# Two attention blocks on one core: gates loaded as one row, first K and V side by side, other buffers and leads, and the last outputs partly projected ahead

## The chip, the cores and the metric

The kernel runs on one core of one Trainium2 chip. The metric is device time in microseconds (us). The kernel before takes 1134.37 us (median of 3 runs, 1133.22 to 1134.79).

The engines are TensorE (PE in the profile; PEld is its weight load), ScalarE (ACT), VectorE (DVE), GpSimd (POOL) and SyncE (SP), which issues most of the DMAs (289 of the 292 in the trace before).

## The reference

Two blocks are computed and their outputs stand side by side, 2048 rows of 1024 each. There are 32 heads of width 32.

```python
# A: plain softmax attention over 2048 keys
qkv = x @ wqkv
p = softmax(q @ k.T * Dh**-0.5);  a = (p @ v) @ wo
# B: 4 segments of 512; causal softmax inside a segment, plus a memory M, z of earlier segments
g = sigmoid(beta)                                  # one gate per head
a_dot = softmax(qs @ ks.T * scale + mask) @ vs
a_mem = (phi(qs) @ M) / (phi(qs) @ z + 1e-6)
o = g * a_mem + (1 - g) * a_dot;  b = concat(o) @ wo
```

## The kernel before

A small list scheduler in Python decides, before the program is built, the order of instructions on every engine. A unit is one query block of 256 rows of one group of four heads (A), or one segment of one group (B). Each unit is cut into score batches: TensorE writes scores into two of three pairs of PSUM banks, and ScalarE takes the exponential of a pair (128x1024) at a time. "Position" (`pos`) counts score batches, and other work is due at a position. The two remaining PSUM banks (`side`) serve everything else: projections, PV and output tiles. PV is the product of the exponentials with V.

```python
par = dict(b=(12, 7, 2), ..., ob=1, lead=5, wob=60, oks=(0, 3), sh=2, od=8, run=6, ...)

def load_misc(self):                       # the gates
    for h in range(4):
        src = bass.AP(tensor=self.B_beta.tensor, offset=self.B_beta.offset + h, ap=[[0, 32], [4, NG]])
        ... e.dma_start(self.beta[32 * h:32 * h + 32, 0:NG], src)      # 32x8 elements of 2 bytes
    yield do("ACT", lambda e: e.activation(gB, self.beta[:, :], ACTF.Exp, scale=-1.0), ...)
    ...

def pv_unit(self, u, steps, half):
    if not self.first_pv:
        self.first_pv = True
        yield ("ev", ("ex", u, 1))         # the first PV goes after two batches of exponentials
    ...
    OB, = yield acq(self.side, 1, -1000)   # and holds a side bank from here on
    ...

def out_A(self, qb):                       # output projection of a query block
    ...                                    # waits for the last two groups of that block
    for tt in range(2):
        for half in range(2):              # 4 tiles of 128x512, 8 groups = 32 matmuls each
            self.Q.spawn(self.out_rows(...))
```

Of the kernel before, what the change touches and what calls it, by code (L numbers as in the profile page):

```python
# [17 lines left out]
NG = 8  # L18
# [153 lines left out]
class Sched:  # L172
# [31 lines left out]
    def step(self, gen, val):  # L204
        while True:
            try:
                req = gen.send(val)
            except StopIteration:
                self.nproc -= 1
                return  # L210
            k = req[0]
            if k == "do":
                rq = req[1]
                rq.proc = gen
                self.seq += 1
                rq.seq = self.seq
                self.q[rq.eng].append(rq)
                self.kick(rq.eng)
                return
            if k == "acq":  # L220
                pool, n, prio, pick = req[1:]
                got = self.take(pool, n, pick)
                if got is not None and not any(x[0] < prio for x in pool.waiting):
                    val = got
                    continue
                if got is not None:
                    pool.items = got + pool.items
                    pool.items.sort()
                self.seq += 1
                pool.waiting.append((prio, self.seq, n, pick, gen))  # L230
                pool.waiting.sort(key=lambda x: x[:2])
                return
            if k == "ev":
                if req[1] in self.events and self.events[req[1]] is True:
                    val = None
                    continue
                self.events.setdefault(req[1], []).append(gen)
                return
            if k == "until":
                if req[1] <= self.now:  # L240
                    val = None
                    continue
                self.at(req[1], lambda g=gen: self.step(g, None))
                return
            raise ValueError(k)
# [10 lines left out]
    def give(self, pool, items):  # L256
        pool.items.extend(items)
        pool.items.sort()
# [119 lines left out]
class Kernel:  # L378
    par = dict(b=(12, 7, 2), mem=-2, memM=2, span=50, rate=0.58, ahead=28, sl=4, pv=24, ob=1, lead=5, b0=1, bpos=16, wob=60, mg=0.05, off=0, oks=(0, 3), sh=2, pd=4, o0=4, od=8, run=6, po=(1, 1), fp=2, fil=0.65, fs=0.15)
# [48 lines left out]
    def alloc(self):  # L428
# [36 lines left out]
        self.beta = sb("beta", [P, 8])  # L465
# [9 lines left out]
    def pt(self, slots):  # L475

        k = slots[0][0]
        i = [s[1] for s in slots]
        step = i[1] - i[0] if len(i) > 1 else 1
        t = (self.PT, self.WoBs, self.OTAs)[k]  # L480
        return t[:, i[0]:i[-1] + 1:step, :]

    def pkey(self, s):
        k, i = s
        if k == 0:
            return ("PT", i)
        return ("WoB", i // 2) if k == 1 else ("OTA", 2 + i // 4, i % 4)
# [14 lines left out]
    def load_xB(self, s):  # L502
        src = self.B_x[0][512 * s:512 * s + 512, :]
        yield do("SP", lambda e: e.dma_start(self.xB[:, :, :], src, transpose=True), w=["xB"], cost=5.2, prio=6, kb=1024)
        self.Q.fire(("xB", s))

    def load_misc(self):
        nc = self.nc
        for h in range(4):
            src = bass.AP(tensor=self.B_beta.tensor, offset=self.B_beta.offset + h, ap=[[0, 32], [4, NG]])  # L510

            def f(e, h=h, src=src):
                with nc.allow_non_contiguous_dma(reason="tiny beta broadcast"):
                    return e.dma_start(self.beta[32 * h:32 * h + 32, 0:NG], src)
            yield do("SP", f, w=[("beta", h)], cost=0.5, prio=8, kb=300)
        gA, gB = self.gcol[:, 0, :], self.gcol[:, 1, :]
        yield do("ACT", lambda e: e.activation(gB, self.beta[:, :], ACTF.Exp, scale=-1.0),
                 r=[("beta", h) for h in range(4)], w=["gcol"], cost=0.2, prio=9)
# [5 lines left out]
    def constants(self):  # L524
# [6 lines left out]
        yield pool(lambda e: e.memset(self.zero[:, :], 0.0), ["zero"])  # L531
        for i in range(2):
# [78 lines left out]
    def rest_x(self):  # L611
        yield ("ev", ("XS", 2))
        yield ("ev", ("XS", 3))
        for c in range(1, 4):
            for t in (0, 2):
# [3 lines left out]
                         r=[("XS", 3), ("XS", 2), ("XS", 1), ("XS", 0)] if c == 1 and t == 0 else [], w=[("xA", c, t), ("xA", c, t + 1)], cost=2.6, prio=1, kb=512)  # L619
# [3 lines left out]
    def job(self, due, mm, keys, out, okey, wkeys, scale=None, eng="DVE", cost=None, okeys=(), gate=None, n=512):  # L623
# [4 lines left out]
        for i in range(last + 1):  # L628
# [4 lines left out]
            if i == 0:  # L633
# [33 lines left out]
    def a_prep(self, g):  # L667
# [16 lines left out]
        if g == 0:  # L684
            todo[0:2] = [("K", 0, 0, 2), ("Q", 0, 0, 2), ("K", 0, 2, 4), ("Q", 0, 2, 4)]
        kind = {"K": 0, "Q": 1, "V": 2}
# [27 lines left out]
        if g == NG - 1:  # L714
            yield do("SP", lambda e: e.dma_start(self.WoA, self.A_wo.rearrange("(j p) n -> p j n", p=P)),
                     w=[("xA", c, t) for c in range(4) for t in range(4)], cost=0.6, prio=5, kb=2048)
            Q.fire("WoA")
        self.nA = g + 1
# [5 lines left out]
    def b_all(self):  # L724
        for n in range(32):
            if n % 8 == 0 and n:
                yield from self.load_xB(n // 8)
            yield from self.b_proj(n)

# [143 lines left out]
    def s_all(self):  # L873
# [6 lines left out]
        pr = yield acq(self.pairs, 1)  # L880
        Q.give(self.side, list(pr[0]))
        pr = yield acq(self.pairs, 1)
        Q.give(self.side, list(pr[0]))

    def s_batch(self, u, k):
# [49 lines left out]
        Q.fire(("pos", self.pos))  # L935
        for x in range(npair):
# [76 lines left out]
    def pv_unit(self, u, steps, half):  # L1013
        Q = self.Q
        if not self.first_pv:
            self.first_pv = True
            yield ("ev", ("ex", u, 1))
# [58 lines left out]
    def finish(self, u, half, OB, tb):  # L1076
# [7 lines left out]
        o = OD[:, 0:QU]  # L1084
        yield do("DVE", lambda e: e.tensor_copy(OD[:, :], self.ps[:, OB, :]), r=[("ps", OB)], w=[("OD", x), ("Rb", x)], cost=dve(2 * QU), prio=0,  # L1085
# [19 lines left out]
        if s == 0:  # L1105
            yield do("DVE", lambda e: e.scalar_tensor_tensor(dst, o, gB, Rb, ALU.mult, ALU.mult),
                     r=[("OD", x), ("Rb", x), "gcol"], w=[("OTB", g, half)], cost=dve(QU) + 0.08, prio=self.par["fp"])
            Q.give(self.ods, [x])
        else:
# [8 lines left out]
                     r=[("tB", tb), ("amem", b)], w=[("OTB", g, half)], cost=dve(QU), prio=self.par["fp"])  # L1118
# [6 lines left out]
    def out_rows(self, due, lhs, lkeys, W, wkey, row, col, gate=None):  # L1125
# [14 lines left out]
        yield do("SP", lambda e: e.dma_start(self.out[0][row:row + P, col:col + 512], self.outsb[ob][:, :]), r=[("outsb", ob)],  # L1140
# [3 lines left out]
    def out_A(self, qb):  # L1144
        yield ("ev", "WoA")
        last = qb == NQ - 1
        for g in (NG - 2, NG - 1):
            if last and g == NG - 1:
                yield ("ev", "s_done")
            else:  # L1150
                yield ("ev", ("fin", "A", g, qb))
        due = self.pos + 4
        for tt in range(2):
            for half in range(2):
                q0 = QU * qb + P * tt
                ns = slice(512 * half, 512 * half + 512)
                self.Q.spawn(self.out_rows(due, lambda j, q0=q0: self.OTA[:, j, q0:q0 + P],
                                           [[("OTA", j, qb // 2)] for j in range(NG)],
                                           lambda j, ns=ns: self.WoA[:, j, ns], [("xA", 0, 0)], q0, 512 * half,
                                           (NG - 1, ("fin", "A", NG - 1, qb)) if last else None))  # L1160
                due += 2
                yield ("until", self.Q.now)
# [199 lines left out]
    def main(self):  # L1362
# [19 lines left out]
        self.extra = [((1, 2 * i), (1, 2 * i + 1)) for i in range(8)] + [((2, 2 * i), (2, 2 * i + 1)) for i in range(8)]  # L1382
# [103 lines left out]
```

## Time and profile before

ScalarE bounds the kernel. These are two lines of the profile's page: the busy time of each engine with its share of the span and its instructions, and the costliest group (line, engine, operation, out<-in, shapes, count | busy, mean ns of one | idle time before them and what ended it).

```profile
PE 1052.7 (93%) x23589; PEld 514.0 (45%) x23589; DVE 720.3 (64%) x1463; ACT 1091.9 (96%) x1190; POOL 132.8 (12%) x286
...
L953 ACT ACTIVATE PT<-ps 128x1024 bf16<-128x1024 f32 x1168 | 1073.0, 1183 | 14.6 <-PE ps L926 14.5
```

With 16 more exponentials that go into borrowed tiles there are 1184. The mean of 1183 ns is the time of one from start to end. They overlap in the trace, where 245 in a row take 0.917 us each, so the cost of one is read from a run of them in the timeline. Below is the timeline of ScalarE before (start us, duration us, engine, line, operation, out<-in, count, and in brackets the idle time ahead of it with what ended it). Consecutive exponentials are merged; every bracket is a hole.

```profile
10.99 1.94 ACT L953 ACTIVATE WoB<-ps 128x1024 bf16<-128x1024 f32 x2 [7.35 <-PE ps L926]
...
42.55 1.94 ACT L953 ACTIVATE PT<-ps 128x1024 bf16<-128x1024 f32 x2 [1.56 <-PE ps L926]
47.14 7.44 ACT L953 ACTIVATE PT<-ps 128x1024 bf16<-128x1024 f32 x8 [2.65 <-PE ps L926]
55.01 5.61 ACT L953 ACTIVATE PT<-ps 128x1024 bf16<-128x1024 f32 x6 [0.44 <-PE ps L926]
62.11 0.21 ACT L517 ACTIVATE gcol<-beta 128x8 f32<-128x8 bf16 x1 [1.49 <-DMA beta<-in_B_beta_dram]
64.86 1.94 ACT L953 ACTIVATE PT<-ps 128x1024 bf16<-128x1024 f32 x2 [2.54 <-PE ps L926]
68.38 42.34 ACT L953 ACTIVATE PT<-ps 128x1024 bf16<-128x1024 f32 x46 [1.58 <-PE ps L926]
...
892.73 224.69 ACT L953 ACTIVATE PT<-ps 128x1024 bf16<-128x1024 f32 x245 [0.91 <-PE ps L926]
1118.91 0.59 ACT L1138 CAST outsb<-ps 128x512 bf16<-128x512 f32 x1 [1.49 <-PE ps L1132]
```

The last run has 245 exponentials in 224.69 us, 0.917 us each. At that pace 1184 exponentials need about 1086 us, and 1088.5 us are what is left of the span of 1132.8 without head, holes and tail. What can be won is the head up to 10.99 us, 17.92 us of holes, and the tail of 15.38 us after the last exponential, which ends at 892.73 + 224.69 = 1117.42 us.

The largest group of holes is at 60 to 68 us. There the timeline of TensorE before shows a stop in the middle of one projection (17 matmuls, then 3 of the next group):

```profile
58.83 1.24 PE L653 MATMUL ps<-xA,WA 128*32 128x512 bf16 x17
...
64.08 0.40 PE L653 MATMUL ps<-xA,WA 128*32 128x512 bf16 x3 [4.01 <-issue]
```

"issue" means that nothing the profile knows of released it. The DMA view of the kernel before for 56 to 60 us has many packets and no bytes to speak of:

```profile
DMA packets 452, 0.00 MB, mean 0 GB/s; under 512 B 452, under 2 KB 452, under 8 KB 452
```

Nearly all of them, 424 of the 452, are the gates: 1024 elements of 2 bytes in four loads, whose packets run from 52.1 to 61.7 us.

### The profile page before, as it was taken

The page shows a single profiled execution, that of the slowest core. Times are in us where ns is not written, and L with a number is a line of the kernel's source. Part 1 is how long each engine was busy: PE and PEld are TensorE (multiplying, and loading weights), DVE is VectorE, ACT ScalarE, POOL GpSimd, SP SyncE. Part 2 cuts the span into 40 slices and gives each one's busy share as a digit, 9 for nine tenths or more (in the row PEclk, how much of TensorE's full clock was granted, in tenths as well). Part 3 has the DMA queues.
Part 4 walks back from the last instruction along what each step waited for, and adds up shares of the span by engine and source line. Part 5 has one row for each costly group of instructions (what it writes and reads, how often), then busy time and mean ns, then how long its engine had stood idle before and what let it go on. Part 6 is the DMA issues. An engine that isn't in the chain of part 4 may idle for free.

```text
span 1132.8 us, 50803 instructions
## 1 busy us (share of the span) xinstructions
PE 1052.7 (93%) x23589; PEld 514.0 (45%) x23589; DVE 720.3 (64%) x1463; ACT 1091.9 (96%) x1190; POOL 132.8 (12%) x286
## 2 busy tenths in 40 slices
PE   7889999999899999999999999999999999999997
PEld 3444444444444444444444444444444444444444
DVE  2237556565784887979767876878567656663333
ACT  5889999999999999999999999999999999999995
POOL 1002102001111111111101201111111111110000
PEclk9999999999999999999999999999999999999999
DMA  9522622224121221254113232232213223211111
GB/s 182 100 46 58 132 54 59 48 55 90 45 45 34 63 59 45 49 69 91 48 40 58 45 60 48 49 77 54 52 42 67 46 40 66 73 22 36 39 40 52
DMA packets 214844, 67.32 MB, mean 59 GB/s; under 512 B 203872, under 2 KB 212064, under 8 KB 214624
## 3 DMA queue, kind: packets, MB, share of 16 engines
q1 hardware_dynamic: 213296, 63.20, 26.7%
q8 instruction: 187, 3.06, 1.2%
q10 hardware_dynamic: 1328, 0.79, 0.3%
q14 instruction: 33, 0.27, 0.1%
HBM read 36.70 MB, written 8.39 MB: 40 GB/s over the span
## 4 chain that ended last, share of the span: by engine, by line
ACT 82%; PE 11%; DVE 3%; DMA 1%; issue 1%; POOL 0%; DVEq 0%
ACT PT L953 81%; PE ps L653 4%; PE ps L1058 3%; PE ps L1132 2%; PE ps L926 2%; DMA VA<-VT 1%; DMA PKt<-PH 1%; DVE OD L1085 0%; ACT OTA L953 0%; PE ps L546 0%; DVE VT L659 0%; DVE we L988 0%; POOL PT L962 0%; ACT WoB L953 0%; DVE we L989 0%
## 5 line engine op out<-in xcount | busy, mean ns | idle before, releaser
L953 ACT ACTIVATE PT<-ps 128x1024 bf16<-128x1024 f32 x1168 | 1073.0, 1183 | 14.6 <-PE ps L926 14.5
L1058 PE MATMUL ps<-PT,ones 128*32 128x256 bf16 (+1 forms) x4800 | 294.7, 271 | 0.0
L1058 PE MATMUL ps<-PT,VA 128*32 128x256 bf16 x4032 | 252.9, 276 | 16.2 <-ACT PT L953 10.4
L926 PE MATMUL ps<-QA,KA 32*128 32x256 bf16 x4096 | 203.9, 273 | 31.9 <-ACT PT L953 22.8
L653 PE MATMUL ps<-xA,WA 128*32 128x512 bf16 (+1 forms) x3136 | 204.3, 378 | 8.5 <-issue 4.6
L653 PE MATMUL ps<-xB,WB 128*32 128x512 bf16 x3072 | 203.1, 381 | 1.1 <-DVE VT L659 0.3
L962 POOL TENSOR_SCALAR_AFFINE_SELECT PT<-PT 128x256 bf16<-128x256 bf16 (+1 forms) x224 | 104.0, 470 | 821.1 <-ACT PT L953 815.8
L926 PEld LDWEIGHTS ps<-QA,KA 32*128 32x128 bf16 x4096 | 60.9, 92 | 204.4 <-ACT PT L953 190.7
L1058 PEld LDWEIGHTS ps<-PT,VA 128*32 128x32 bf16 x4032 | 107.6, 96 | 87.0 <-issue 30.2
L1058 PEld LDWEIGHTS ps<-PT,ones 128*32 128x32 bf16 x4800 | 128.8, 97 | 25.1 <-issue 0.3
L653 PEld LDWEIGHTS ps<-xA,WA 128*32 128x32 bf16 x3136 | 72.9, 96 | 82.4 <-issue 29.0
L1138 DVE CAST outsb<-ps 128x512 bf16<-128x512 f32 x60 | 41.4, 689 | 100.0 <-PE ps L1132 99.9
L653 PEld LDWEIGHTS ps<-xB,WB 128*32 128x32 bf16 x3072 | 72.5, 96 | 70.0 <-issue 25.8
L1085 DVE COPY OD<-ps 128x512 f32<-128x512 f32 x128 | 87.3, 683 | 24.7 <-PE ps L1058 23.6
L659 DVE CAST KQB<-ps 128x512 bf16<-128x512 f32 x64 | 44.0, 688 | 76.1 <-PE ps L653 75.9
L659 DVE CAST VT<-ps 128x512 bf16<-128x512 f32 x64 | 44.0, 688 | 75.8 <-PE ps L653 73.0
L1132 PE MATMUL ps<-WoB,OTB 128*32 128x512 bf16 x1024 | 66.8, 381 | 0.1
L1132 PE MATMUL ps<-xA,OTA 128*32 128x512 bf16 x1024 | 65.6, 381 | 0.0
L1091 DVE STREAM_TRANSPOSE OD<-Rall 128x256 f32<-128x256 f32 x128 | 56.3, 441 | 3.4
L1088 DVE STREAM_TRANSPOSE Dt<-OD 128x256 f32<-128x256 f32 x128 | 55.8, 437 | 2.5
L1058 PE MATMUL ps<-PT,VB 128*32 128x256 bf16 (+1 forms) x768 | 45.6, 260 | 7.6 <-DVE OD L1085 3.8
L926 PE MATMUL ps<-KQB 32*128 32x128 bf16 (+3 forms) x512 | 43.0, 302 | 3.9 <-ACT PT L953 2.8
(77 smaller groups left out, 654.7 us busy)
## 6 DMA issues: line engine op xcount, KB each, us to landing
WB<-in_B_wk_dram SPq DMA_DIRECT2D x32, 256.0 KB, 2.9
WB<-in_B_wq_dram SPq DMA_DIRECT2D x32, 256.0 KB, 2.9
WB<-in_B_wv_dram SPq DMA_DIRECT2D x32, 256.0 KB, 3.3
out_dram<-outsb SPq DMA_DIRECT2D x64, 128.0 KB, 1.8
WA<-in_A_wqkv_dram SPq DMA_DIRECT2D x23, 256.0 KB, 3.2
WoB<-in_B_wo_dram SPq DMA_DIRECT2D x1, 2048.0 KB, 10.3
xA<-in_A_wo_dram SPq DMA_DIRECT2D x1, 2048.0 KB, 10.4
OTA<-in_A_x_dram ACTq DMA_DIRECT2D x2, 256.0 KB, 4.9
```

Source lines behind the costliest of these rows:

```text
L653: ins = e.matmul(self.ps[32 * c:32 * c + 32, bank, 0:n], W[:, i, 32 * c:32 * c + 32], x(i), start=(i == 0), stop=(i == NI - 1))
L659: return e.tensor_copy(dst, self.ps[:, bank, 0:n])
L926: ins = e.matmul(self.ps[:, bk, col:col + w], lhs(t, hs), rhs(q0, w, hs), start=True, stop=True)
L953: yield do("ACT", lambda e: e.activation(ap, self.ps[:, pr[0]:pr[1] + 1, :], ACTF.Exp, scale=sc), r=[("ps", bk) for bk in pr], w=keys, cos ...
L962: yield do("POOL", lambda e, m=m, n=n: e.affine_select(m, m, pattern=[[0, n], [1, P]], compare_op=ALU.is_ge, fill=0.0, base=0, channel_mul ...
L1058: ins = e.matmul(out, l, r, start=st, stop=sp)
L1085: yield do("DVE", lambda e: e.tensor_copy(OD[:, :], self.ps[:, OB, :]), r=[("ps", OB)], w=[("OD", x), ("Rb", x)], cost=dve(2 * QU), prio=0 ...
L1088: yield do("DVE", lambda e: e.transpose(Dt[:, :], Rb), r=[("Rb", x)], w=[("Dt", x)], cost=dve(QU), prio=self.par["fp"], hold=0.15)
L1091: yield do("DVE", lambda e: e.transpose(Rb.rearrange("p (a b) -> p a b", b=32), self.spread(Rc)), r=[("Rc", ui % 64)], w=[("Rb", x)], cost ...
L1132: ins = e.matmul(self.ps[32 * c:32 * c + 32, bank, :], lhs(j)[:, 32 * c:32 * c + 32], W(j), start=(j == 0), stop=(j == NG - 1))
L1138: return f(self.outsb[ob][:, :], self.ps[:, bank, :])
```

## The change

The intent is to take away what stands between ScalarE and its next exponential. The gates come as one row and TensorE spreads them. The first group's V projections run beside its K and Q projections, and the first PV waits until V is whole (`pvw`). B's projections are due earlier (`b`). Eight more places for exponentials (an exponential of 128x1024 takes two) are lent by B's output tile. Six of the last eight output tiles are projected over seven groups ahead of time into f32 partial sums, and only the last group is added at the end.

```diff
-    par = dict(b=(12, 7, 2), ..., ob=1, lead=5, wob=60, oks=(0, 3), sh=2, od=8, run=6, ...)
+    par = dict(b=(16, 12, 9), ..., ob=4, lead=6, wob=40, oks=(1,), sh=6, od=4, run=4, ..., ta=2, td=40, pvw=3)
@@ pools: first in, first out
-        pool.items.sort()
@@ load_misc
-        for h in range(4): ... four strided loads of 32x8 elements
+        yield do("SP", lambda e: e.dma_start(self.beta[0:1, :], self.B_beta.rearrange("(o h) -> o h", o=1)), ...)
+            for h in range(4):
+                ins = e.matmul(self.ps[32 * h:32 * h + 32, bank, 0:NG], self.ones32[:, :], self.beta[:, h:32:4], start=True, stop=True)
+        yield do("ACT", lambda e: e.activation(gB, self.ps[:, bank, 0:NG], ACTF.Exp, scale=-1.0), ..., prio=-2)
@@ a_prep
+        if g == 0:
+            streams = [[t for t in todo if t[0] != "V"], [t for t in todo if t[0] == "V"]]
@@ pv_unit
-            yield ("ev", ("ex", u, 1))
+            yield ("ev", ("VA", 0, self.par["pvw"]))
@@ main
+        self.extra = ... + [((3, 2 * i), (3, 2 * i + 1)) for i in range(4)]        # places in OTB
@@ finish: the last unit is normalised straight from PSUM
+        if u == ("A", NG - 1, NQ - 1): ...
@@ out_ahead (new): groups 0 to 6 now, group 7 later
+        yield from self.job(d, mm, ..., lambda e, bank, eng: e.tensor_copy(part, self.ps[:, bank, :]), [("part", i)] + over, ...)
+        yield ("ev", ("fin", "A", NG - 1, qb))
+        yield from self.job(-99, lambda e, j, bank: mm(e, NG - 1, bank, True), ...,
+                            lambda e, bank, eng: e.tensor_tensor(self.outsb[ob][:, :], self.ps[:, bank, :], part, ALU.add), ...)
```
(Cut: keys, costs, transfer sizes that only the scheduler's model uses, `out_A`'s choice of tiles, and one output DMA issued from ScalarE.)

More of the change, by code (lines that the diff above doesn't have):

```diff
@@ L257, in give @@
         pool.items.extend(items)
-        pool.items.sort()
         while pool.waiting:
@@ L378 @@
 class Kernel:
-    par = dict(b=(12, 7, 2), mem=-2, memM=2, span=50, rate=0.58, ahead=28, sl=4, pv=24, ob=1, lead=5, b0=1, bpos=16, wob=60, mg=0.05, off=0, oks=(0, 3), sh=2, pd=4, o0=4, od=8, run=6, po=(1, 1), fp=2, fil=0.65, fs=0.15)
+    par = dict(b=(16, 12, 9), mem=-2, memM=2, span=50, rate=0.58, ahead=28, sl=4, pv=24, ob=4, lead=6, b0=1, bpos=16, wob=40, mg=0.05, off=0, oks=(1,), sh=6, pd=4, o0=4, od=4, run=4, po=(1, 1), fp=2, fil=0.65, fs=0.15, ta=2, td=40, pvw=3)
     def __init__(self, nc, A_x, A_wqkv, A_wo, B_x, B_wq, B_wk, B_wv, B_wo, B_beta, out):
@@ L464, in alloc @@
         self.we = sb("we", [P, 512], F32)
-        self.beta = sb("beta", [P, 8])
+        self.beta = sb("beta", [P, 32])
         self.gcol = sb("gcol", [P, 2, 8], F32)
@@ L479, in pt @@
         step = i[1] - i[0] if len(i) > 1 else 1
-        t = (self.PT, self.WoBs, self.OTAs)[k]
+        t = (self.PT, self.WoBs, self.OTAs, self.OTB)[k]
         return t[:, i[0]:i[-1] + 1:step, :]
@@ L486, in pkey @@
             return ("PT", i)
+        if k == 3:
+            return ("OTB", i)
         return ("WoB", i // 2) if k == 1 else ("OTA", 2 + i // 4, i % 4)
@@ L503, in load_xB, with f @@
         src = self.B_x[0][512 * s:512 * s + 512, :]
-        yield do("SP", lambda e: e.dma_start(self.xB[:, :, :], src, transpose=True), w=["xB"], cost=5.2, prio=6, kb=1024)
+        yield do("SP", lambda e: e.dma_start(self.xB[:, :, :], src, transpose=True), w=["xB"], cost=5.2, prio=6, kb=1500)
         self.Q.fire(("xB", s))
     def load_misc(self):
-        nc = self.nc
-        for h in range(4):
-            src = bass.AP(tensor=self.B_beta.tensor, offset=self.B_beta.offset + h, ap=[[0, 32], [4, NG]])
-            def f(e, h=h, src=src):
-                with nc.allow_non_contiguous_dma(reason="tiny beta broadcast"):
-                    return e.dma_start(self.beta[32 * h:32 * h + 32, 0:NG], src)
-            yield do("SP", f, w=[("beta", h)], cost=0.5, prio=8, kb=300)
+        yield do("SP", lambda e: e.dma_start(self.beta[0:1, :], self.B_beta.rearrange("(o h) -> o h", o=1)), r=["beta0"], w=["beta"], cost=0.5,
+                 prio=8, kb=10)
+        bank, = yield acq(self.side, 1, self.first[("B", 0)])
+        def f(e):
+            for h in range(4):
+                ins = e.matmul(self.ps[32 * h:32 * h + 32, bank, 0:NG], self.ones32[:, :], self.beta[:, h:32:4], start=True, stop=True)
+            return ins
+        yield do("PE", f, r=["beta", "ones32"], w=[("ps", bank)], cost=0.1, prio=8, mode=COL)
         gA, gB = self.gcol[:, 0, :], self.gcol[:, 1, :]
-        yield do("ACT", lambda e: e.activation(gB, self.beta[:, :], ACTF.Exp, scale=-1.0),
-                 r=[("beta", h) for h in range(4)], w=["gcol"], cost=0.2, prio=9)
+        yield do("ACT", lambda e: e.activation(gB, self.ps[:, bank, 0:NG], ACTF.Exp, scale=-1.0), r=[("ps", bank)], w=["gcol"], cost=0.25, prio=-2)
+        self.Q.give(self.side, [bank])
         yield do("DVE", lambda e: e.tensor_scalar(gB, gB, 1.0, None, ALU.add), r=["gcol"], w=["gcol"])
@@ L531, in constants @@
         yield pool(lambda e: e.memset(self.zero[:, :], 0.0), ["zero"])
+        yield pool(lambda e: e.memset(self.beta[:, :], 0.0), ["beta0"])
         for i in range(2):
@@ L618, in rest_x @@
                 yield do("SP", lambda e, q0=q0, src=src: e.dma_start(self.xA[:, :, q0:q0 + 2 * P], src, transpose=True),
-                         r=[("XS", 3), ("XS", 2), ("XS", 1), ("XS", 0)] if c == 1 and t == 0 else [], w=[("xA", c, t), ("xA", c, t + 1)], cost=2.6, prio=1, kb=512)
+                         r=[("XS", 3), ("XS", 2), ("XS", 1), ("XS", 0)] if c == 1 and t == 0 else [], w=[("xA", c, t), ("xA", c, t + 1)], cost=2.6, prio=1, kb=680)
             self.Q.fire(("xA", c))
@@ L632, in job @@
                      prio=(lambda: self.jprio(due)) if i == 0 else (lambda: min(self.jprio(due), self.par["run"])), mode=COL)
-            if i == 0:
+            if i == 0 and last:
                 self.under.add(bank)
@@ L685, in a_prep, with a_stream @@
             todo[0:2] = [("K", 0, 0, 2), ("Q", 0, 0, 2), ("K", 0, 2, 4), ("Q", 0, 2, 4)]
+        if g == 0:
+            streams = [[t for t in todo if t[0] != "V"], [t for t in todo if t[0] == "V"]]
+        else:
+            streams = [todo]
+        for i, st in enumerate(streams):
+            Q.spawn(self.a_stream(g, st, due, ("stream", g, i)))
+        for i in range(len(streams)):
+            yield ("ev", ("stream", g, i))
+        if g == NG - 1:
+            yield do("SP", lambda e: e.dma_start(self.WoA, self.A_wo.rearrange("(j p) n -> p j n", p=P)),
+                     w=[("xA", c, t) for c in range(4) for t in range(4)], cost=0.6, prio=5, kb=2048)
+            Q.fire("WoA")
+        self.nA = g + 1
+    def a_stream(self, g, todo, due, done):
+        Q = self.Q
+        b = g % 2
         kind = {"K": 0, "Q": 1, "V": 2}
@@ L713, in a_prep @@
                 Q.spawn(self.load_WA(k, g + 1))
-        if g == NG - 1:
-            yield do("SP", lambda e: e.dma_start(self.WoA, self.A_wo.rearrange("(j p) n -> p j n", p=P)),
-                     w=[("xA", c, t) for c in range(4) for t in range(4)], cost=0.6, prio=5, kb=2048)
-            Q.fire("WoA")
-        self.nA = g + 1
+        Q.fire(done)
     def v_turn(self, b, c, vt, g):
@@ L728, in b_all @@
             yield from self.b_proj(n)
+        self.Q.fire("xBfree")
     def b_proj(self, n):
@@ L879, in s_all @@
         Q.fire("s_done")
-        pr = yield acq(self.pairs, 1)
-        Q.give(self.side, list(pr[0]))
-        pr = yield acq(self.pairs, 1)
-        Q.give(self.side, list(pr[0]))
+        for _ in range(3):
+            pr = yield acq(self.pairs, 1)
+            Q.give(self.side, list(pr[0]))
     def s_batch(self, u, k):
@@ L935, in s_batch @@
         Q.fire(("pos", self.pos))
+        if u == ("A", NG - 2, NQ - 1) and k == 7:
+            Q.fire("K6")
         for x in range(npair):
@@ L1084, in finish @@
         o = OD[:, 0:QU]
+        if u == ("A", NG - 1, NQ - 1):
+            o = self.ps[:, OB, 0:QU]
+            yield do("DVE", lambda e: e.transpose(Dt[:, :], self.ps[:, OB, QU:2 * QU]), r=[("ps", OB)], w=[("Dt", x)], cost=dve(QU), prio=-5, hold=0.15)
+            yield do("DVE", lambda e: e.reciprocal(Rc, Dt[:, 0:QU:32]), r=[("Dt", x)], w=[("Rc", ui % 64)], cost=0.15, prio=-5, hold=0.15)
+            yield do("DVE", lambda e: e.transpose(Rb.rearrange("p (a b) -> p a b", b=32), self.spread(Rc)),
+                     r=[("Rc", ui % 64)], w=[("Rb", x)], cost=dve(QU), prio=-5, hold=0.15)
+            g, qb = u[1], u[2]
+            yield do("DVE", lambda e: e.tensor_tensor(self.OTA[:, g, QU * qb:QU * qb + QU], o, Rb, ALU.mult),
+                     r=[("ps", OB), ("Rb", x)], w=[("OTA", g, qb // 2)], cost=dve(QU), prio=-5)
+            Q.fire(("rc", ui))
+            Q.give(self.side, [OB])
+            Q.fire(("fin", "A", g, qb))
+            return
         yield do("DVE", lambda e: e.tensor_copy(OD[:, :], self.ps[:, OB, :]), r=[("ps", OB)], w=[("OD", x), ("Rb", x)], cost=dve(2 * QU), prio=0,
@@ L1106, in finish @@
             yield do("DVE", lambda e: e.scalar_tensor_tensor(dst, o, gB, Rb, ALU.mult, ALU.mult),
-                     r=[("OD", x), ("Rb", x), "gcol"], w=[("OTB", g, half)], cost=dve(QU) + 0.08, prio=self.par["fp"])
+                     r=[("OD", x), ("Rb", x), "gcol"], w=[("OTB", g, half), ("OTB", g)], cost=dve(QU) + 0.08, prio=self.par["fp"])
             Q.give(self.ods, [x])
@@ L1117, in finish @@
             yield do("DVE", lambda e: e.tensor_tensor(dst, tB[:, :], self.amem[b][:, QU * half:QU * half + QU], ALU.add),
-                     r=[("tB", tb), ("amem", b)], w=[("OTB", g, half)], cost=dve(QU), prio=self.par["fp"])
+                     r=[("tB", tb), ("amem", b)], w=[("OTB", g, half), ("OTB", g)], cost=dve(QU), prio=self.par["fp"])
             Q.give(self.tbs, [tb])
@@ L1123, in finish, with out_rows @@
                 Q.spawn(self.out_B(s))
-    def out_rows(self, due, lhs, lkeys, W, wkey, row, col, gate=None):
+    def out_rows(self, due, lhs, lkeys, W, wkey, row, col, gate=None, via="SP"):
         Q = self.Q
@@ L1139, in out_rows @@
         yield from self.job(due, mm, lkeys, out, [("outsb", ob)], wkey, eng="any", gate=gate)
-        yield do("SP", lambda e: e.dma_start(self.out[0][row:row + P, col:col + 512], self.outsb[ob][:, :]), r=[("outsb", ob)],
+        yield do(via, lambda e: e.dma_start(self.out[0][row:row + P, col:col + 512], self.outsb[ob][:, :]), r=[("outsb", ob)],
                  cost=0.5, prio=4, kb=128)
@@ L1144, in out_A @@
     def out_A(self, qb):
+        Q = self.Q
         yield ("ev", "WoA")
-        last = qb == NQ - 1
-        for g in (NG - 2, NG - 1):
-            if last and g == NG - 1:
-                yield ("ev", "s_done")
-            else:
-                yield ("ev", ("fin", "A", g, qb))
-        due = self.pos + 4
-        for tt in range(2):
-            for half in range(2):
-                q0 = QU * qb + P * tt
-                ns = slice(512 * half, 512 * half + 512)
-                self.Q.spawn(self.out_rows(due, lambda j, q0=q0: self.OTA[:, j, q0:q0 + P],
-                                           [[("OTA", j, qb // 2)] for j in range(NG)],
-                                           lambda j, ns=ns: self.WoA[:, j, ns], [("xA", 0, 0)], q0, 512 * half,
-                                           (NG - 1, ("fin", "A", NG - 1, qb)) if last else None))
-                due += 2
-                yield ("until", self.Q.now)
+        yield ("ev", ("fin", "A", NG - 2, qb))
@@ new lines, in out_A @@
+        parts = [(tt, half) for tt in range(2) for half in range(2)]
+        if qb >= NQ - 2:
+            ahead = parts if qb == NQ - 2 else parts[:self.par["ta"]]
+            for i, (tt, half) in enumerate(ahead):
+                Q.spawn(self.out_ahead(qb, tt, half, i if qb == NQ - 2 else 4 + i))
+            parts = parts[len(ahead):]
+        last = qb == NQ - 1
+        yield ("ev", "s_done" if last else ("fin", "A", NG - 1, qb))
+        due = self.pos + 4
+        for i, (tt, half) in enumerate(parts):
+            q0 = QU * qb + P * tt
+            ns = slice(512 * half, 512 * half + 512)
+            Q.spawn(self.out_rows(due, lambda j, q0=q0: self.OTA[:, j, q0:q0 + P], [[("OTA", j, qb // 2)] for j in range(NG)],
+                                  lambda j, ns=ns: self.WoA[:, j, ns], [("xA", 0, 0)], q0, 512 * half,
+                                  (NG - 1, ("fin", "A", NG - 1, qb)) if last else None, "ACT" if last and i % 2 else "SP"))
+            due += 2
+            yield ("until", Q.now)
@@ new lines, in out_ahead, with mm @@
+    def out_ahead(self, qb, tt, half, i):
+        Q = self.Q
+        yield ("ev", "xBfree" if i < 4 else "K6")
+        t, over = ((self.xB, ["xB"]), (self.KA[0], [("KA", 0, k) for k in range(8)]), (self.QA[0], [("QA", 0, k) for k in range(8)]))[max(0, i // 2 - 1)]
+        t = t[:, :, :].rearrange("p a b -> p (a b)").bitcast(F32) if i < 4 else t[:, :].bitcast(F32)
+        lo = 512 * (i if i < 4 else i % 2)
+        part = t[:, lo:lo + 512]
+        q0 = QU * qb + P * tt
+        ns = slice(512 * half, 512 * half + 512)
+        lhs = lambda j: self.OTA[:, j, q0:q0 + P]
+        def mm(e, j, bank, only=False):
+            for c in range(4):
+                ins = e.matmul(self.ps[32 * c:32 * c + 32, bank, :], lhs(j)[:, 32 * c:32 * c + 32], self.WoA[:, j, ns],
+                               start=(j == 0 or only), stop=(j == NG - 2 or only))
+            return ins
+        d = len(self.order) - self.par["td"] + i
+        yield from self.job(d, mm, [[("OTA", j, qb // 2)] for j in range(NG - 1)], lambda e, bank, eng: e.tensor_copy(part, self.ps[:, bank, :]),
+                            [("part", i)] + over, [("xA", 0, 0)])
+        yield ("ev", ("fin", "A", NG - 1, qb))
+        ob, = yield acq(self.outs, 1, d)
+        yield from self.job(-99, lambda e, j, bank: mm(e, NG - 1, bank, True), [[("OTA", NG - 1, qb // 2)]],
+                            lambda e, bank, eng: e.tensor_tensor(self.outsb[ob][:, :], self.ps[:, bank, :], part, ALU.add),
+                            [("outsb", ob)], [("xA", 0, 0)], okeys=[("part", i)])
+        row, col = q0, 512 * half
+        yield do("SP", lambda e: e.dma_start(self.out[0][row:row + P, col:col + 512], self.outsb[ob][:, :]), r=[("outsb", ob)], cost=0.5, prio=4, kb=128)
+        Q.give(self.outs, [ob])
@@ L1381, in main @@
         self.slots = Pool([((0, 2 * i), (0, 2 * i + 1)) for i in range(RING // 2)])
-        self.extra = [((1, 2 * i), (1, 2 * i + 1)) for i in range(8)] + [((2, 2 * i), (2, 2 * i + 1)) for i in range(8)]
+        self.extra = [((1, 2 * i), (1, 2 * i + 1)) for i in range(8)] + [((2, 2 * i), (2, 2 * i + 1)) for i in range(8)] + [((3, 2 * i), (3, 2 * i + 1)) for i in range(4)]
         self.order = self.batches()
```

## The prediction

> **What bounds it now.** ScalarE. The page's busy table has ACT at 1091.9 of 1132.8 us (96%), PE at 93%, DVE at 64%. The groups show 1184 exponentials of 128x1024; ScalarE's timeline gives 245 of them in 224.69 us, 0.917 us each, so about 1088 us in all, and the change takes none away (its "places" are buffers for results, in OTB). The rest, 45 us, is all that can be won:
> - head: the first exponential starts at 10.99 us;
> - holes between exponentials, 18 us: about 2 before 28 us; 4.65 from 41 to 55 us; 5.8 from 60.6 to 68.4 us; 5.7 scattered after that;
> - tail: the last exponential ends at 1117.42, so 15.4 us.
>
> **Gates (beta).** ScalarE waits 1.49 us for the beta DMA and runs the small activation for 0.21. Then it waits 2.54 for scores, because PE stands still from 60.07 to 64.08 with releaser "issue" in the middle of a projection. In that stretch the DMA view has almost only beta's 2-byte packets (about 1000, little bandwidth used), and an instruction packet arrives just before PE resumes. I read it as an instruction fetch held up behind beta. [...] After it matmuls of 256 columns take 0.44 us instead of 0.28, and ScalarE waits 1.58 more. One 64-byte row and four tiny matmuls should remove nearly all this: -5.6 us.
>
> **First K and V, pvw, OTB places.** Holes of 1.56, 2.65 and 0.44 us come at 42 to 55 us: PE is in order and stands before a PV matmul that needs a V transpose landing at 45.66, with score matmuls behind it. In the changed instruction order all four first V projections and three V transposes come earlier, 14 score batches (before: 10) precede the first PV, and PV starts only when V is whole. The second score batch now stands behind 64 instead of 32 matmuls, which costs perhaps 0.6 us, mostly recovered in the next two holes. Net -3.5 us (-1 to -4.5).
>
> **Last outputs ahead.** After the last PV, PE runs 172 output matmuls (9.36 us in the timeline, 0.055 each); then 0.58 eviction and 4.65 to the end of the span. The changed order has 136 left there, not a handful: PE is already 97% busy in the last 100 us, so taking six partial tiles forward pushes other tiles back. -2 us. The finish chain read straight from PSUM is hidden by those matmuls: 0.
>
> **Longer leads for B, queues first-in first-out.** They can close some of the 5.7 us of scattered holes (1.45 us before 269 us, 1.03 before 584 us): -1.5 us, uncertain in sign.
>
> **Sum.** 1134.4 - 5.6 - 3.5 - 2.0 - 1.5 = 1121.8 us; say 1122, eight times in ten between 1116 and 1129. Over 2% faster would need 1111.7: nearly every hole and half the tail. Chances: faster 0.05, within 2% 0.94, slower 0.01.
>
> **What will show each step.** ScalarE busy stays near 1092. Beta: no 4 us "issue" stall of PE near 60 us and ScalarE without a hole over 1 us from 55 to 70 us. K/V: the sum of holes from 30 to 55 us at most 2 us. Tail: last exponential to end of span about 13.4 us, with PE busy to about 5 us before the end. The first exponential still starts at 11 us.
>
> **What would make it wrong.** The PE stall is another fetch problem (after the large xB transpose) and returns; the last V transpose lands late, so that the delayed PV opens a hole of several us; the longer leads make B's projections crowd scores in the middle; the partial sums' extra evictions delay PSUM banks near the end, and holes appear before the last exponential.

That an instruction fetch is held up is the reading of one trace: the 4.01 us stop, the 2-byte packets meanwhile, and the instruction packet that moved from 61.61 to 62.58 us, 1.5 us before TensorE resumed at 64.08. The first experiments test it.

## The result, and the profile after

The changed kernel takes 1120.09 us (median of 4 runs, 1119.13 to 1120.85), against 1134.58 us for the kernel before on the same chip. A ratio is the mean time of one kernel's runs over that of the other's of the same rounds, so it isn't quite the ratio of the medians; here it is 0.9873, with a 95% interval of 0.9856 to 0.9890. Outputs are correct.

The page after: ScalarE's busy time is the same and its share is 98%.

```profile
PE 1045.8 (94%) x23493; PEld 512.1 (46%) x23493; DVE 726.3 (65%) x1467; ACT 1091.2 (98%) x1191; POOL 134.8 (12%) x287
...
L970 ACT ACTIVATE PT<-ps 128x1024 bf16<-128x1024 f32 x1164 | 1068.4, 1202 | 2.6 <-PE ps L941 2.4
```

The timeline of ScalarE after, same columns:

```profile
10.38 1.94 ACT L970 ACTIVATE WoB<-ps 128x1024 bf16<-128x1024 f32 x2 [6.59 <-PE ps L941]
13.24 5.61 ACT L970 ACTIVATE WoB<-ps 128x1024 bf16<-128x1024 f32 x6 [0.93 <-PE ps L941]
21.43 7.44 ACT L970 ACTIVATE OTA<-ps 128x1024 bf16<-128x1024 f32 x8 [2.58 <-PE ps L941]
...
50.27 8.36 ACT L970 ACTIVATE PT<-ps 128x1024 bf16<-128x1024 f32 x9 [0.98 <-PE ps L941]
58.42 0.28 ACT L518 ACTIVATE gcol<-ps 128x8 f32<-128x8 f32 x1
58.48 84.56 ACT L970 ACTIVATE PT<-ps 128x1024 bf16<-128x1024 f32 x92
...
400.97 702.67 ACT L970 ACTIVATE PT<-ps 128x1024 bf16<-128x1024 f32 x766 [0.56 <-PE ps L941]
```

The gates' activation has no hole before or after it, and from 401 us to the last exponential, 766 in a row, there is no hole at all. The table sums the brackets of both timelines by stretch (us).

| stretch | before | after | difference | predicted |
|---|---|---|---|---|
| up to the first exponential | 10.99 | 10.38 | -0.6 | 0 |
| holes up to 30 us | 1.97 | 3.51 | +1.5 | 0.6, mostly recovered |
| holes 30 to 56 us | 4.65 | 0.98 | -3.7 | -3.5 with the line above |
| holes 56 to 110 us | 5.61 | 0.00 | -5.6 | -5.6 |
| holes after 110 us | 5.69 | 1.40 | -4.3 | -1.5 |
| after the last exponential | 15.38 | 13.76 | -1.6 | -2.0 |
| exponentials themselves (the rest) | 1088.5 | 1087.4 | -1.1 | 0 |
| span | 1132.8 | 1117.4 | -15.4 | -12.6 |

The first exponential starts between 9.85 and 11.33 us in all profiles, before and after alike, so 0.6 us there is no effect. The tail of one profile is no better than 1.5 us: with the changed kernel's last instructions it is 13.5 to 13.8 us in five profiles and 15.3 in two, with those of the kernel before 15.4 to 15.6 in three. The 2.58 us hole at 21 us, ahead of the fifth score batch, is new: the changed order puts two score batches in a row ahead of a projection, and TensorE ran the projection slowly. The timeline of TensorE after:

```profile
14.41 0.40 PE L941 MATMUL ps<-QA,KA 32*128 32x256 bf16 x8 [1.22 <-ACT WoB L970]
16.16 0.61 PE L941 MATMUL ps<-QA,KA 32*128 32x256 bf16 x8 [1.34 <-ACT WoB L970]
16.70 4.35 PE L655 MATMUL ps<-xA,WA 128*32 128x512 bf16 x52
```

52 matmuls took 4.35 us here; they take 2.99 us in the last experiment below.

Some other holes go with the clock records of the traces (PEclk) too. In the kernel before TensorE's clock is at 0.50 from 64.9 to 68.3 us, right after the 4 us stop, and the 1.58 us hole at 68.38 ends this stretch. It is at 0.50 again from 266.3 to 269.7, and the largest of the scattered holes, 1.45 us at 269.46, lies there. A profile of the same order of TensorE (`before_double_beta`) has no such stretch there and no such hole, and 4.20 us of holes after 110 us in place of 5.69. The changed kernel has a second stretch at 285.7 to 289.2 us, with a hole of 0.34. So of the line "holes after 110 us" more than 1 us may be where the clock happened to fall.

### The profile page after: what moved, and what is told of

The parts are those of the page before. It is cut to its first block, busy times and chain, and to the rows that moved or that the text cites. A ratio compares the mean times of both kernels' runs of the same rounds, so it can differ in the third digit from the quotient of the medians.

```text
span 1117.4 us, 50583 instructions
## 1 busy us (share of the span) xinstructions
PE 1045.8 (94%) x23493; PEld 512.1 (46%) x23493; DVE 726.3 (65%) x1467; ACT 1091.2 (98%) x1191; POOL 134.8 (12%) x287
## 4 chain that ended last, share of the span: by engine, by line
ACT 88%; PE 7%; DVE 2%; DMA 1%; SPq 1%; issue 0%; DVEq 0%
ACT PT L970 87%; PE ps L655 3%; PE ps L1075 1%; PE ps L941 1%; PE ps L1162 1%; SPq L504 1%; DVE VT L661 0%; PE ps L548 0%; DMA PKt<-PH 0%; DMA VB<-VT 0%; ACT OTB L970 0%; ACT WoB L970 0%; DVE we L1006 0%; DVE ue L1002 0%; PE ps L590 0%
## 5 line engine op out<-in xcount | busy, mean ns | idle before, releaser
L1075 PE MATMUL ps<-PT,ones 128*32 128x256 bf16 (+1 forms) x4784 | 290.3, 270 | 0.0
L1075 PE MATMUL ps<-PT,VA 128*32 128x256 bf16 x4016 | 248.6, 275 | 11.2 <-ACT PT L970 7.5
L1168 DVE CAST outsb<-ps 128x512 bf16<-128x512 f32 x53 | 36.6, 691 | 77.9 <-PE ps L1162 77.6
L1162 PE MATMUL ps<-xA,OTA 128*32 128x512 bf16 x832 | 53.6, 381 | 0.0
```

What stands on the lines that cost most here:

```text
L1075: ins = e.matmul(out, l, r, start=st, stop=sp)
L1162: ins = e.matmul(self.ps[32 * c:32 * c + 32, bank, :], lhs(j)[:, 32 * c:32 * c + 32], W(j), start=(j == 0), stop=(j == NG - 1))
L1168: return f(self.outsb[ob][:, :], self.ps[:, bank, :])
```

## The experiments

Twelve kernels ran, all correct. "Hole" is again idle time of ScalarE ahead of an exponential.

### The gates alone, on the kernel before

```diff
-        for h in range(4): ... four strided loads          (before)
+        one load of a row, four matmuls, activation from PSUM   (the changed kernel's load_misc)
```

> The kernel before with the gates alone loaded as one row and spread by TensorE. Descriptor theory: TensorE's 4.01 us stop near 60 us is an instruction fetch behind beta's 2-byte packets, so it goes, and with it ScalarE's holes of 1.49, 2.54 and 1.58 us; the time falls by about 5.6 us to 1129 us. Rival, that the fetch is held up by the large transpose of B's input whatever beta does: the stop stays at 3 us or more and the time falls by under 2 us.

Measured: 1129.21 us, ratio to before 0.9942 (0.9913 to 0.9971), so about 6.6 us less (3.3 to 9.9 by the interval). The 4 us stop is gone, the longest "issue" wait of TensorE in the first 110 us is 0.68 us, and there is no hole from 57 to 106 us. So the gates alone give what was put down to them, as far as the interval can tell. The scattered holes stayed (5.1 us from 110 to 900 us, 5.7 before), so they have another cause.

### The old loads twice, on the kernel before

```diff
             yield do("SP", f, w=[("beta", h)], cost=0.5, prio=8, kb=300)
+        for h in range(4): ... the same four loads into self.beta2, which nothing reads
```

> The kernel before with beta's four loads issued twice, the second four into a tile that nothing reads; the order of instructions on TensorE is the same. Descriptor theory: the packets take twice as long to pass, TensorE's stop grows from 4 us to between 8 and 11 us, and the time rises by 4 to 7 us. Rival (the transpose is the cause): the stop stays near 4 us and the time does not change by more than 1.5 us.

Measured: 1140.28 us, ratio 1.0042 (1.0013 to 1.0070), 4.4 to 4.8 us more. TensorE's order is unchanged, and its stop grew from 4.01 to 11.41 us at the same instruction. Timeline of TensorE in this kernel:

```profile
58.47 1.24 PE L661 MATMUL ps<-xA,WA 128*32 128x512 bf16 x17
71.12 0.61 PE L661 MATMUL ps<-xA,WA 128*32 128x512 bf16 x3 [11.41 <-issue]
```

### The old loads added to the changed kernel

```diff
+        for h in range(4): ... the four old loads into self.beta2, right after the new one
```

> The changed kernel with the old four beta loads added into a tile that nothing reads, right after the new one; the order on TensorE is that of the changed kernel. Descriptor theory: a stop of TensorE of about 4 us with releaser issue comes back between 48 and 65 us and costs 3 to 6 us (1123 to 1126 us). [...] Rival: no stop over 1.5 us, time within 1 us of the changed kernel's 1120.

Measured: 1127.08 us, ratio to before 0.9923 (0.9893 to 0.9952), against 0.9873 without them. The time is above the 1123 to 1126 expected. TensorE's order is that of the changed kernel to the last instruction; the trace also has holes of 1.10 and 0.78 us at half clock (108.7 and 295.9 us) and one of the long tails (15.3 us). A stop appeared at another instruction, a score batch this time. Timelines of TensorE and of ScalarE in this kernel:

```profile
59.66 0.39 PE L953 MATMUL ps<-QA,KA 32*128 32x256 bf16 x2 [4.34 <-issue]
```

```profile
60.09 1.94 ACT L982 ACTIVATE PT<-ps 128x1024 bf16<-128x1024 f32 x2 [4.37 <-PE ps L953]
```

The three runs agree: the 2-byte loads stop TensorE, the longer the more of them there are (four 4.01 and 4.34 us, eight 11.41, and without them the longest "issue" wait in the first 110 us is 0.68 and 1.07), and in either program.

That what is held up is the fetch of instructions is an inference from the traces' lists of packets and instructions. In the kernel before one queue (q8, whose kind the profile gives as "instruction") moved 187 packets of 16 KB, 3.06 MB. TensorE's recorded instructions, weight loads included, are 47401. If all these packets are TensorE's, about 253 instructions go to a packet (an estimate from these two counts). The stop falls on the same place of that stream in all three programs that have it: 1985 recorded instructions of TensorE precede it. With the gates as one row a packet of q8 starts at 57.64 us, 4.3 after the one ahead of it. With the old loads the next packet starts only when the 2-byte packets run out, at 61.61 (they end at 61.67), and in the changed kernel with the old loads at 57.29 (57.42). With the loads doubled it starts at 68.94, late in packets that last until 70.87. TensorE resumes 1.2 to 1.5 us after this packet has moved. How the small packets hold up this queue is not shown.

The rival has a small share: in the changed kernel TensorE still stops for 1.07 us with "issue" at 49.95 us, and that is the 0.98 us hole at 50 us. There 1729 instructions precede, 256 fewer than at the longer stop, about one packet by the estimate above, and the packet of q8 starts at 47.43, when the large transpose of B's input, whose packets end between 47 and 48 us, is nearly done.

### The old tail in the changed kernel

```diff
-    def out_A ... out_ahead ...            (partial sums)
+    def out_A ...                          (the old one; also the old last normalisation)
```

> The changed kernel with the old output projection for the last two query blocks and the old last normalisation (the partial sums ahead of the last group taken out). Theory from the two traces: the time from the end of the last exponential to the end of the span goes back from 13.8 to about 15.4 us, so the time rises by about 1.6 us; holes of ScalarE before that stay within 1 us. Rival, that the partial sums also free TensorE time before the end and so closed scattered holes: the time rises by over 3 us with new holes between 900 us and the last exponential.

Measured: 1124.78 us, ratio 0.9903 (0.9875 to 0.9932). The tail is 18.64 us, not the 15.4 expected, and the holes are unchanged (6.03 us in all, none after 900). With the new settings the old tail leaves 224 output matmuls after the last PV, where the kernel before left 172. So the new settings alone make the tail longer, and the partial sums with the new last normalisation, which no run takes apart, give back 4.9 us, of which 1.6 remain against before.

### The new tail in the kernel before

```diff
+    def out_ahead, the new out_A and the last normalisation from PSUM; settings of before, ta=2, td=40
```

> The kernel before with the partial sums ahead of the last group and the last normalisation read from PSUM alone; its own settings otherwise. After the last PV this leaves 116 output matmuls in TensorE's order instead of 172. Theory (after the last exponential TensorE works off what is left at 0.055 us a matmul, and about 6 us more follow): the tail falls from 15.4 to about 12.3 us, the time by about 3 us to 1131. Rival (moving them forward only moves the wait): new holes of ScalarE after 1000 us eat the gain and the time falls by under 1 us.

Measured: 1134.69 us, ratio 0.9994 (0.9965 to 1.0023): nothing. The tail fell by only 1.0 us, to 14.38, and 2.05 us of new holes opened at 1074 to 1086 us. The last ScalarE copy waited 2.18 us for an output DMA to free its buffer, so the count of matmuls (116 left) alone did not rule there. The rival's forecast held: what the work saved at the end came back as holes where it had been brought forward.

### One stream again

```diff
-        if g == 0:
-            streams = [[t for t in todo if t[0] != "V"], [t for t in todo if t[0] == "V"]]
+        streams = [todo]
```

> The changed kernel with the first group's K, Q and V projections in one stream again, in the old order; everything else changed. Theory (side by side streams bring the V transposes forward): the last V transpose lands later, and ScalarE's holes from 30 to 56 us rise from 1.0 to 2.5 us or more, time 1121.5 to 1124. Rival (the wait of the first PV for the whole of V, kept here, is what closed them): holes there stay within 1 us of the changed kernel's 1.0 and the time within 1.5 us of 1120.

Measured: 1121.23 us (1118.74 to 1124.94), ratio 0.9904 (0.9876 to 0.9932); the profiled run has a span of 1117.2 us, that of the changed kernel. Holes from 30 to 56 us are 2.34 us against 0.98. Neither forecast was met in full (2.5 us or more; within 1 us of 1.0). The side by side streams are worth about 1.4 us in that stretch of the trace, and the times cannot tell it from zero.

### The first PV let go early

```diff
-            yield ("ev", ("VA", 0, self.par["pvw"]))
+            yield ("ev", ("ex", u, 1))
```

> The changed kernel with the first PV again let go as soon as the second batch of exponentials of its unit is done, so that PV matmuls stand in TensorE's queue before V is whole. Theory (in-order TensorE behind a V transpose makes the holes): 2 to 5 us of holes come back between 30 and 56 us, time 1122 to 1125. Rival (the streams alone closed them): holes there stay within 1 us of 1.0.

Measured: 1129.52 us, ratio 0.9961 (0.9944 to 0.9978), which is about 9 us slower than the changed kernel, twice what was expected. Timeline of TensorE, VectorE, SyncE and ScalarE in this kernel:

```profile
44.16 6.35 SPq L504 DMA_TRANSPOSE xB<-in_B_x_dram  x1
44.80 0.40 PE L941 MATMUL ps<-QA,KA 32*128 32x256 bf16 x8 [0.53 <-ACT PT L970]
...
47.53 0.69 DVE L661 CAST VT<-ps 128x512 bf16<-128x512 f32 x1 [3.06 <-PE ps L655]
49.51 3.02 PE L572 MATMUL ps<-maskbd,zero 128*32 128x256 bf16 x103 [0.19 <-issue]
50.55 1.27 SPq L667 DMA_TRANSPOSE VA<-VT  x1
...
56.37 0.40 PE L941 MATMUL ps<-QA,KA 32*128 32x256 bf16 x8
...
56.82 3.77 ACT L970 ACTIVATE PT<-ps 128x1024 bf16<-128x1024 f32 x4 [9.41 <-PE ps L941]
```

V's last block leaves PSUM at 47.53 us; in the changed kernel it does at 35.40. Its transpose is then issued only at 50.55, after B's large one, and no score batch runs from 44.80 to 56.37. The code says how V got late: a PV that has begun holds one of the two side banks, and the projections have to share the other. That step is read from code and order; no run isolates it. It holds for the changed order only: the kernel before also lets the first PV go early, and its holes from 30 to 56 us are 4.65 us in all.

### Without the places in B's output tile

```diff
-        self.extra = ... + [((3, 2 * i), (3, 2 * i + 1)) for i in range(4)]
+        self.extra = ...
```

> The changed kernel without the eight extra places for exponentials in the output tile of B. TensorE's order is the same but for the place names, so I expect no change: holes from 30 to 60 us within 0.5 us of the changed kernel's, time within 1 us. If the places matter, ScalarE or TensorE waits for a place to be read by PV, and a hole of 1 to 4 us appears between 36 and 50 us.

Measured: 1120.07 us, ratio 0.9885 (0.9867 to 0.9902). The holes from 30 to 56 us are 0.55 us. The places do nothing: TensorE's order is the same without them and nothing waits for a place. This profile's tail is 15.25 us with the same order; the issue of one output DMA took 2.23 us instead of 0.43 in it.

### B's old leads

```diff
-    par = dict(b=(16, 12, 9), ...
+    par = dict(b=(12, 7, 2), ...
```

> The changed kernel with B's projections again due 12, 7 and 2 score batches ahead instead of 16, 12 and 9. Theory (late B projections make the scattered holes): the holes between 110 us and the end go back from 1.4 to 4 to 6 us and the time rises by 2.5 to 4.5 us. Rival (they closed through the first-in first-out pools or by chance of the new order): holes after 110 us stay below 2.5 us.

Measured: 1128.76 us, ratio 0.9953 (0.9937 to 0.9970), about 9 us slower than the changed kernel, again more than expected. Holes after 110 us are 11.80 us, and one makes most of it. Timeline of TensorE, VectorE and ScalarE:

```profile
843.52 0.40 PE L941 MATMUL ps<-QA,KA 32*128 32x256 bf16 x8
...
850.20 0.69 DVE L661 CAST KQB<-ps 128x512 bf16<-128x512 f32 x1
...
853.15 0.69 DVE L661 CAST KQB<-ps 128x512 bf16<-128x512 f32 x1 [2.27 <-PE ps L655]
...
853.90 0.39 PE L941 MATMUL ps<-KQB 32*128 32x512 bf16 x4 [0.36 <-DVE KQB L661]
...
854.34 1.94 ACT L970 ACTIVATE PT<-ps 128x1024 bf16<-128x1024 f32 x2 [8.26 <-PE ps L941]
```

Score batches go in a fixed order. The next one belonged to a B unit whose K and Q left PSUM only at 850.9 and 853.8 us, so all scores waited. The longer leads are what keeps this hole out of the changed kernel. The kernel before has the short leads without that one hole, so the other settings matter with them.

### Partial sums due earlier

```diff
-    par = dict(..., ta=2, td=40, pvw=3)
+    par = dict(..., ta=2, td=60, pvw=3)
```

> The changed kernel with the partial sums due 60 score batches before the end instead of 40; the matmuls left after the last PV fall from 136 to 104. Theory of the count: tail 12.0 us instead of 13.8, time about 1118. Rival (they crowd TensorE earlier): holes of ScalarE after 900 us rise from 0 to 1 us or more and the time stays at 1120.

Measured: 1120.25 us, ratio 0.9883 (0.9863 to 0.9904). Both theories hold at once: the tail is 11.90 us, as the count said, and 1.90 us of holes opened at 1025 and 1027 us. The timeline of TensorE and ScalarE shows the first of them:

```profile
1020.89 0.40 PE L941 MATMUL ps<-QA,KA 32*128 32x256 bf16 x8
...
1022.75 1.69 PE L1210 MATMUL ps<-xA,OTA 128*32 128x512 bf16 x28
1024.36 0.40 PE L941 MATMUL ps<-QA,KA 32*128 32x256 bf16 x8
...
1024.81 1.94 ACT L970 ACTIVATE PT<-ps 128x1024 bf16<-128x1024 f32 x2 [1.23 <-PE ps L941]
```

A whole partial tile of 28 matmuls stands between two score batches, which are 3.47 us apart; two exponentials take 1.83.

### Four tiles ahead in the last block

```diff
-    par = dict(..., ta=2, td=40, pvw=3)
+    par = dict(..., ta=4, td=60, pvw=3)
```

> The changed kernel with all four tiles of the last query block summed ahead, due 60 score batches before the end; 48 output matmuls are left after the last PV. By the count alone the tail would be 6.2 + 48 x 0.055 = 8.9 us, but now the last normalisation (1.9 us after the last PV) and four additions of 0.69 us on VectorE in a row should bind: tail 10 to 11 us, time about 1117. If the count alone rules, under 9.3; if the additions or holes cost more than they save, the time is 1119 or above.

Measured: 1122.93 us, ratio 0.9906 (0.9887 to 0.9925), slower than the changed kernel. The tail is 13.78 us, not 10 to 11, and the holes after 900 us are 3.01 us. In this order 120 output matmuls follow the last score batch, but 72 of them stand ahead of the last PV, so the last normalisation begins 3.0 us after the last exponential instead of 1.5. Counting only what comes after the last PV overlooked them.

### TensorE kept busy in front of the two early batches

```diff
+        if self.pos == 2:
+            self.wbank = (yield acq(self.side, 1, -100))[0]
+        if self.pos in (2, 3):
+            yield self.warm(4, self.wbank)      # 4 matmuls of 512 columns, result unused
+        if self.pos == 3:
+            Q.give(self.side, [self.wbank])
```

> The changed kernel with four idle-filling matmuls of 512 columns ahead of the third score batch and four ahead of the fourth, into a spare PSUM bank that nothing reads; the rest of TensorE's order is the same. In seven of nine profiles of the changed kernel and its variants TensorE's granted clock fell to about half from 16 to 20 us after it had stood in front of these two batches, and ScalarE then had a hole of 2.1 to 3.9 us at 21 us; in the two with the clock up the hole was 1.0. Theory (the idle time drops the clock): clock 1.00 from 16 to 20 us, hole at 20 to 22 us of 1.0 or less, time down by 1 to 2 us to about 1118.5. Rival (the input's transposes arriving late make the hole): the clock is up but the hole stays at 2 us or more and the time at 1120.

Measured: 1117.35 us (4 runs, 1115.49 to 1117.80), ratio to before 0.9854 (0.9831 to 0.9877). Busy time and granted clock by stretch (start:end, length, PE busy with instructions, PEclk, DMA share, GB/s) in the changed kernel, then in this one:

```profile
14.00:16.00 2.00, 0.40 (x8) 1.00 1.30 260
16.00:18.00 2.00, 1.84 (x24) 0.52 1.29 261
18.00:20.00 2.00, 2.00 (x28) 0.62 1.53 98
```

```profile
14.00:16.00 2.00, 1.58 (x20) 1.00 1.14 247
16.00:18.00 2.00, 2.00 (x44) 1.00 1.28 266
18.00:20.00 2.00, 2.00 (x40) 1.00 1.17 106
```

```profile
16.00 2.99 PE L655 MATMUL ps<-xA,WA 128*32 128x512 bf16 x52
```

The clock stayed at 1.00, the 52 matmuls took 2.99 us (last fence, its timeline), and the hole is 1.06 us in place of 2.58, just above the 1.0 expected. Only eight matmuls were added to the order. This is the fastest version. It ran in another call than the changed kernel and their intervals overlap, so the trace, not the two times, carries the claim that it is better. The trace is one profile, so chance is not ruled out; and it has no stretch at half clock before the end at all, so a part of its shorter span (1113.8 against 1117.4 us), the missing hole near 288 us for one, is not shown to be the eight matmuls' doing. What the clock goes by is not shown. Two of nine profiles kept it up without any help (1.00 from 14 to 20 us in `after_no_otb` and `tail_ta4_td60`). In the traces of the kernel before and the changed one each stretch at half clock before the last exponential lasts 3.41 us, two in each; in others it is that or about twice or four times that. The fall at 64.92 us in the kernel before followed the 4.01 us stop, but in the changed kernel TensorE was not idle for as long: ahead of the fall at 16.09 us its longest idle stretch was 1.34 us, and it was busy for 0.91 of the last 3.41 us; ahead of the fall at 285.75 us it was busy for 2.07 of them. How busy it must be to keep the clock was not measured.

## Why the prediction was right

The time, 1120.09 us, lies in the range (1116 to 1129), and the gain of 14.5 us is near the forecast of 12.4 (1134.4 to 1122). That the sum came so near owes something to luck: the first K and V gave 1.3 us less than forecast, the stretch after 110 us 2.8 more, and 1.7 (the start and the exponentials themselves) was not forecast at all. Point by point:

- **Bound.** Right: ScalarE's busy time went from 1091.9 to 1091.2 us, and the gain is all in holes and tail.
- **Gates.** Right in size (-5.6 us) and in cause. Three runs put the load on, off and doubled: a stop of 4.34, none, and 11.41 us. The 1.58 us that ScalarE waits after it, which the prediction counted, goes with the half clock that followed the stop (0.50 from 64.9 to 68.3 us).
- **First K and V.** The forecast of -3.5 us was net of the start; measured so it is -2.2 (-3.7 at 30 to 56 us and +1.5 before), inside its range of -1 to -4.5. The mechanism is right only in part. The prediction had TensorE standing in order before a PV; that wait is 1.14 us in the trace of before, where TensorE sat idle from 44.56 to 45.70 us until the transpose had landed, and the score batch behind the PV began only at 46.69, though ScalarE was out of work from 44.49 and the queries had left PSUM at 45.31. What counts more in the changed order is when the first PV begins: let go early it costs about 9 us, and V's projections come late. The streams are worth about 1.4 us in the trace, the places in B's output tile nothing.
- **Second score batch.** The prediction gave it 0.6 us, mostly recovered, and that came true: its hole is 0.93 us against 0.66, and the holes of 0.59, 0.36 and 0.36 that followed are gone. The start still lost 1.5 us, through the hole ahead of the fifth batch, which the prediction does not have. In the three profiles with the clock up (the last experiment and two others) it is 1.0 to 1.1 us and the start loses nothing against before; so the loss goes with TensorE's halved clock (0.52 from 16 to 18 us in the changed kernel, 1.00 in those three).
- **Tail.** The size was right (-1.6 against -2.0, where a profile is good to 1.5), and 136 matmuls left was the reason given for a small gain. In before, changed, old tail and earlier sums, 172, 136, 224 and 104 matmuls left gave tails of 15.38, 13.76, 18.64 and 11.90 us: (18.64 - 11.90) / (224 - 104) = 0.056 us for each. Two runs are off that line: 116 left gave 14.38 us, and 48 gave 13.78. And the term isn't the partial sums' own: alone on the kernel before they gain nothing, and without them and the new last normalisation the changed kernel's tail is 18.64.
- **Longer leads and the pools.** This term of the sum was mis-sized: -1.5 against -4.3 us, and "uncertain in sign" was too cautious; of the -4.3 more than 1 may be the clock. With the old leads 10.4 us of holes come back, so the sign is shown. What the first-in first-out pools do was not tried alone, nor were the other settings one by one, and it stays open how they share the rest.

## What to carry to other kernels

Count what the bounding engine waits for, stretch by stretch, and predict from that; where work is only moved, ask what the second busiest engine does in the place it goes to. TensorE, 96.5% busy in the kernel before from 1017 to 1117 us, gave the work back as holes: 2.05 us with the new tail in that kernel, 1.90 us with the earlier partial sums in the changed one. A load of a few bytes can be dear when it is made of a thousand elements, as the gates were (four loads of 0.5 KB took 4.9 to 9.8 us to land, and TensorE stopped for 4.01 us meanwhile): look for stops that no semaphore explains, and load a row and spread it on the chip. A wait put in on purpose can be worth more than the work it delays, here about 9 us; the likely reason is that beginning early means holding a bank that others need. And look at the clock in each stretch before a hole is put down to the order of work.
